# Attention blocks ahead of and beside a gated product: sums issued before maxima, four copies moved to ScalarE, the mask added on TensorE

## The chip, the core and the metric

The kernel runs on one core of one Trainium2 chip. The metric is the device time of one launch in microseconds. The engines are TensorE (matmuls, PE; its weight loads are PEld), VectorE (DVE), ScalarE (ACT), GpSimd (POOL) and the queue of SyncE (SP), from which most loads are issued. Each engine works through its own instructions in the order in which the kernel issues them.

## The reference

Three layers follow each other; all tensors are float32.

```
scores = q @ k^T / 8, only where 0 <= row - column < 64, else -1e9
attn   = exp(scores - max) / (sum(exp(scores - max)) + 1e-9);  x = attn @ v     # 4 x 8 heads, 576 rows, 64 wide
h = x @ w_in;  g = h * tanh(softplus(h));  y = g @ w_out                       # 2304 tokens, 512 -> 2048 -> 512
each token goes to its best of 8 experts: out = weight * relu(y @ w1[e]) @ w2[e]  # 512 -> 1024 -> 512
```

Since a row looks back over 64 columns at most, 64 rows need 128 columns of keys.

## The kernel before

The 2304 tokens make 36 attention blocks of 64 rows (`a`). A block holds all eight heads: four tiles (`KD`) of 128 x 128 scores, each with two heads on its 128 partitions. A block passes through stages that lie in different steps of the program (`na` counts the steps):

- `scores(a)`, step a: four float32 matmuls into one PSUM tile (L143). For a < 12 (`PRE`) a matmul of an identity with a bfloat16 mask is added ahead of them (L141), so the tile is already masked.
- `largest(a)`, step a+1: the row maxima. For a < 12 one DVE reduction over 128 x 512 in PSUM (L158) and a small POOL instruction that scales it (L159). From block 12 on, four DVE instructions of 128 x 128 each (L165), which add the mask, scale, write the result to SBUF and keep the minimum; they need no POOL instruction, and they free the PSUM tile.
- `exps(a)`, step a+1: four ACT exponentials, with the sums in `sm` (L183). For a < 12 they read PSUM, so the tile stays taken until they end.
- `scale(a)`, step a+2 (`LN`): a small POOL addition to the sums (L197), a DVE reciprocal (L198) and four POOL multiplications of 128 x 128 (L200).
- `flip(a)`, `flipped(a)`, `values(a)`, step a+3 (`LT`): four PE transposes (L210), a copy of their PSUM tile to SBUF (L215, by ACT for the steps in `PT_ACT`, else by DVE), eight pairs of products with v (L226).
- `done(a)`, step a+4: ACT copies the result out of PSUM (L238 or L244); for the first eight blocks `rest` takes a low part on DVE (L251).

Steps 0 to 11 are **attention alone** (`att_alone`). Its order is: loads, `done`, `largest(na-1)`, `scale(na-2)`, `flip(na-3)`, `scores(na)`, `flipped`, `rest`, `exps(na-1)`, conversions, `values(na-3)`. The conversions turn the 64-bit input weights of the gated layer into a high and a low 32-bit part: three DVE instructions (L299, L303, L307), an ACT cast (L325) and a DVE subtraction (L1003) for each of 32 pieces.

Then follow 28 **mixed** steps, one for each product step i of the gated layer: `hidden(i)` (24 matmuls into one of two PSUM tiles `h`; L337 to L341), `att_a`, the output product of step i-2 (12 matmuls; L376 to L378), `att_b`. The activation of h is spread over ACT and DVE: `mish_a` in `att_b` (L414 to L419), `mish_b` in the next `att_a` (`finish_mish`; L425 to L427), then the split of its result (L433, L434). L427 is the last reader of `h`; with two such tiles, `hidden(i)` waits for L427 of step i-2. In mixed steps `att_a` holds `largest(na-1)` and `scale(na-2)` ahead of `finish_mish`, and `scores(na)` is last in `att_b`. Conversions run until product step 13 (`CONV_END`).

Blocks with a < 12 alternate between two PSUM places for their scores; later blocks share one (`att_ps`, one buffer). The transposes of blocks from 9 on and all results `o` share another. The order is written out by hand (`manual_schedule`): no planner moves an instruction.

Of the kernel before, what the change touches and what calls it, by code (L numbers as in the profile page):

```python
# [11 lines left out]
F32 = mybir.dt.float32  # L12
# [12 lines left out]
P = 128  # L25
# [8 lines left out]
NB = NT // BLK  # L34
G = 256
NG = NT // G
KD = D // P
NEG = -8.0e9
LN, LT = 2, 3
PRE = 12  # L40
AHEAD = 1
PT_ACT = range(PRE, 27)
RAW_AT = -1, 1, 3
V_AT = 1
REST = range(NG)
# [24 lines left out]
class Attention:  # L70
# [59 lines left out]
    def scores(self, a):  # L130
        nc = self.nc
        g, j = divmod(a, 2)
        if a % 2 and a < PRE:
            s = self.spare.tile([P, KD, P], F32, name="s_acc", tag="acc1")
        else:
            s = self.ps.tile([P, KD, P], F32, name="s")
        masked = a < PRE
        if masked:
            mask = self.c["mask0_b"] if a % (S // BLK) == 0 else self.c["mask_b"]
            mask = mask.unsqueeze(1).broadcast_to([P, KD, P])  # L140
            nc.tensor.matmul(s, self.eye, mask, start=True, stop=False)  # L141
        for c in range(KD):
            nc.tensor.matmul(  # L143
                s[:, c, :],
                self.qd[g % 2][:, c].rearrange("p h (q j) -> p j (h q)", j=2)[:, j],
                self.kt[g][:, c, j * BLK : j * BLK + P],
                start=not masked,
                stop=not masked or c == KD - 1,
            )
        self.s[a] = s  # L150

    def largest(self, a):

        nc = self.nc
        s = self.s.pop(a)
        mx = self.pp.tile([P, KD], F32, name="mx")
        if a < PRE:
            nc.vector.tensor_reduce(out=mx, in_=s, op=ALU.max, axis=AX.X)  # L158
            nc.gpsimd.tensor_scalar(mx, mx, -1.0 / math.sqrt(HD), None, ALU.mult)  # L159
            self.p[a] = s, mx, 1.0 / math.sqrt(HD)  # L160
            return
        p = self.pp.tile([P, KD, P], F32, name="p")
        mask = self.c["mask0"] if a % (S // BLK) == 0 else self.c["mask"]
        for c in range(KD):
            nc.vector.tensor_tensor_reduce(  # L165
                out=p[:, c, :],
                in0=s[:, c, :],
                in1=mask,
                scale=-1.0 / math.sqrt(HD),
                scalar=3.0e38,  # L170
                op0=ALU.add,
                op1=ALU.min,
                accum_out=mx[:, c : c + 1],
            )
        self.p[a] = p, mx, -1.0

    def exps(self, a):
        nc = self.nc
        s, nm, scale = self.p[a]
        p = self.pp.tile([P, KD, P], F32, name="p") if a < PRE else s  # L180
        sm = self.pp.tile([P, KD], F32, name="sm")
        for c in range(KD):
            nc.scalar.activation(  # L183
                p[:, c, :],
                s[:, c, :],
                AF.Exp,
                scale=scale,
                bias=nm[:, c : c + 1],
                accum_out=sm[:, c : c + 1],
            )  # L190
        self.p[a] = p, sm
# [72 lines left out]
STEPS_ATT = NB + LT + 1  # L264
# [667 lines left out]
def tile_kernel(tc, a):  # L932
    nc = tc.nc
    with ExitStack() as ctx:
# [22 lines left out]
        with tc.manual_schedule():  # L957
# [4 lines left out]
            A = Attention(nc, att_ctx, tc, a["qT"], a["kT"], a["v"], a["x"], c, R.acc_ps, R.first_x)  # L962
# [21 lines left out]
            def convert_start(n):  # L984
                for _ in range(n):
                    if not under_way:
                        if not todo:
                            return
                        under_way.append((todo[0], R.convert_a(R.raws.pop(todo.pop(0)))))
                    key, parts = under_way[0]  # L990
                    f = next(parts)
                    if f is not None:
                        under_way.clear()
                        half_done.append((key, f))
                        fetch_next()
# [3 lines left out]
            def convert_end():  # L999
                def low():  # L1000
                    while low_parts:
                        key, args = low_parts.pop(0)
                        nc.vector.tensor_tensor(*args)  # L1003
                        ready.add(key)

                low()
                while half_done:
                    key, f = half_done.pop(0)
                    low_parts.append((key, R.convert_b(key, f)))
                if not todo and not under_way:  # L1010
                    low()

            na = 0

            def pt_copy():
                if na in PT_ACT:
                    return nc.scalar.copy
                return nc.vector.tensor_copy

            def att_a(convs, *between):  # L1020
                if A.on(na - LT - 1):
                    A.done(na - LT - 1)
                convert_end()
                convert_start(convs)
                if na < STEPS_ATT:
                    A.fetch(na)
                if A.on(na - 1):
                    A.largest(na - 1)
                if A.on(na - LN):
                    A.scale(na - LN)  # L1030
                A.rest()
                for f in between:
                    f()
                if A.on(na - LT):
                    A.flip(na - LT)

            def att_b(convs, *between):
                nonlocal na
                if A.on(na - LT):
                    A.flipped(na - LT, pt_copy())  # L1040
                convert_end()
                convert_start(convs)
                for f in between:
                    f()
                if A.on(na - 1):
                    A.exps(na - 1)
                if A.on(na - LT):
                    A.values(na - LT)
                if na < NB:
                    A.scores(na)  # L1050
                na += 1

            def att_alone(convs):
                nonlocal na
                A.fetch(na)
                if A.on(na - LT - 1):
                    A.done(na - LT - 1)
                if A.on(na - 1):
                    A.largest(na - 1)
                if A.on(na - LN):  # L1060
                    A.scale(na - LN)
                if A.on(na - LT):
                    A.flip(na - LT)
                A.scores(na)
                if A.on(na - LT):
                    A.flipped(na - LT, pt_copy())
                A.rest()
                if A.on(na - 1):
                    A.exps(na - 1)
                convert_end()  # L1070
                convert_start(convs)
                if A.on(na - LT):
                    A.values(na - LT)
                na += 1
# [14 lines left out]
            for i in range(PRE):  # L1089
                att_alone(PRE_CONV[i])  # L1090
                for _ in range(RAW_AT.count(i)):
                    fetch_next()
# [116 lines left out]
            for i in range(n + LAG):  # L1209
# [16 lines left out]
                if i < MIXED:  # L1226
                    att_a(CONV, finish_mish)
                else:
                    finish_mish()
# [34 lines left out]
                if i < MIXED:  # L1264
                    att_b(CONV, start_mish)
                else:
                    start_mish()
# [97 lines left out]
```

## Time and profile before

| | |
|---|---|
| median of 3 runs | 757.12 us (755.93 to 757.47) |
| profiled execution | 757.77 us, span 756.1 us |
| PE busy | 725.9 us, 96% |
| DVE busy | 557.0 us, 74% |
| ACT busy | 490.7 us, 65% |
| POOL busy | 244.2 us, 32% |
| mean granted TensorE clock | 0.995 |

Busy time is the time in which an engine runs instructions other than register, branch, semaphore and DMA-issuing ones. A share over the whole span says little here, since the stages have different limits. The first product step of the gated layer starts 45.10 us into the span; the mixed steps with conversions end near 157 us.

### The profile page before, as it was taken

The page shows a single profiled execution, that of the slowest core. Times are in us where ns is not written, and L with a number is a line of the kernel's source. Part 1 is how long each engine was busy: PE and PEld are TensorE (multiplying, and loading weights), DVE is VectorE, ACT ScalarE, POOL GpSimd, SP SyncE. Part 2 cuts the span into 40 slices and gives each one's busy share as a digit, 9 for nine tenths or more (in the row PEclk, how much of TensorE's full clock was granted, in tenths as well). Part 3 has the DMA queues.
Part 4 walks back from the last instruction along what each step waited for, and adds up shares of the span by engine and source line. Part 5 has one row for each costly group of instructions (what it writes and reads, how often), then busy time and mean ns, then how long its engine had stood idle before and what let it go on. Part 6 is the DMA issues. An engine that isn't in the chain of part 4 may idle for free. (4 is left out here: it accounts for less than half of the span.)

```text
span 756.1 us, 14103 instructions
## 1 busy us (share of the span) xinstructions
PE 725.9 (96%) x5109; PEld 647.6 (86%) x5109; DVE 557.0 (74%) x1389; ACT 490.7 (65%) x1018; POOL 244.2 (32%) x319
## 2 busy tenths in 40 slices
PE   6779999999999999999999999999989999999995
PEld 4568888888989899989988999988879998899994
DVE  4889999975655589889889898999895447643330
ACT  4568888898687677777777777776123546545461
POOL 5763333432323010110101101051424566565661
PEclk9999999999999999999999999999999999999998
DMA  8776666632322310100101001242011711111620
GB/s 267 246 227 232 208 209 220 221 119 78 109 87 72 126 31 1 56 17 15 57 1 57 15 15 64 78 148 75 29 57 56 264 43 44 42 56 43 206 74 32
DMA packets 42912, 75.51 MB, mean 100 GB/s; under 512 B 3857, under 2 KB 20241, under 8 KB 42706
## 3 DMA queue, kind: packets, MB, share of 16 engines
q1 hardware_dynamic: 30818, 56.01, 23.2%
q0 software_dynamic: 4480, 14.46, 5.7%
q10 hardware_dynamic: 7536, 4.06, 1.9%
q8 instruction: 42, 0.69, 0.4%
q14 instruction: 36, 0.29, 0.1%
HBM read 82.36 MB, written 13.39 MB: 127 GB/s over the span
## 5 line engine op out<-in xcount | busy, mean ns | idle before, releaser
L337 PE MATMUL h<-xh,w 128*128 128x256 f32 x576 | 165.9, 288 | 0.8 <-DVE y L427 0.5
L341 PE MATMUL h<-xh,w 128*128 128x256 f32 x576 | 162.8, 283 | 0.0
L340 PE MATMUL h<-xl,w 128*128 128x256 f32 x576 | 162.8, 283 | 0.0
L376 PE MATMUL acc<-w,g 128*128 128x512 f32 x288 | 115.5, 401 | 0.0
L337 PEld LDWEIGHTS h<-xh,w 128*128 128x128 f32 x576 | 110.0, 191 | 6.0 <-DVE y L427 3.3
L377 PE MATMUL acc<-w,g 128*128 128x512 f32 x288 | 112.7, 391 | 0.0
L378 PE MATMUL acc<-w,g 128*128 128x512 f32 x288 | 112.6, 391 | 0.0
L340 PEld LDWEIGHTS h<-xl,w 128*128 128x128 f32 x576 | 110.2, 191 | 1.4
L200 POOL TENSOR_SCALAR p<-p,r 128x128 f32<-128x128 f32 x144 | 84.2, 601 | 80.9 <-DVE r L198 80.9
L341 PEld LDWEIGHTS h<-xh,w 128*128 128x128 f32 x576 | 110.1, 191 | 0.0
L549 DVE CUSTOM_DVE_ANT_0 junk<-row,wg 128x512 bf16<-128x512 f32 x144 | 105.7, 734 | 2.7
L628 POOL DMA_INDIRECT xs_dram<-row,posi x18 | 20.3, 1127 | 215.2 <-DVE row L619 97.2
L873 POOL TENSOR_TENSOR ew<-s,ew 128x1024 fp32r<-128x1024 f32 x32 | 80.0, 2514 | 27.7 <-ACT ew L872 27.5
L441 ACT ACTIVATE g<-h 128x512 fp32r<-128x512 f32 x36 | 21.5, 598 | 100.9 <-PE h L341 100.9
L340 PE MATMUL h<-xl,ew 128*128 128x256 f32 x288 | 82.5, 286 | 1.5 <-DVE xl L907 1.5
L337 PE MATMUL h<-xh,ew 128*128 128x256 f32 x288 | 82.3, 286 | 0.5 <-DVE g L442 0.5
L341 PE MATMUL h<-xh,ew 128*128 128x256 f32 x288 | 82.2, 285 | 0.0
L414 ACT ACTIVATE y<-h 128x512 f32<-128x512 f32 x72 | 43.0, 597 | 56.9 <-PE h L341 53.7
L419 DVE SCALAR_TENSOR_TENSOR pq<-y,r 128x512 f32<-128x512 f32 x72 | 49.9, 693 | 36.7 <-ACT r L417 36.7
L865 DVE TENSOR_TENSOR ew<-s,ew 128x1024 fp32r<-128x1024 f32 x32 | 55.1, 1721 | 25.3 <-ACT ew L864 25.1
L442 DVE SCALAR_TENSOR_TENSOR g<-h,g 128x512 fp32r<-128x512 f32 x36 | 24.8, 689 | 62.4 <-ACT g L441 62.3
L425 ACT ACTIVATE pq<-pq,mid 128x512 f32<-128x512 f32 x72 | 52.1, 723 | 27.5 <-DVE pq L419 23.3
(216 smaller groups left out, 1704.3 us busy)
## 6 DMA issues: line engine op xcount, KB each, us to landing
s<-e_w SPq DMA_DIRECT2D x32, 1024.0 KB
v<-v SPq DMA_DIRECT2D x36, 256.0 KB
raw<-w_in SPq DMA_DIRECT2D x16, 512.0 KB
raw<-w_out SPq DMA_DIRECT2D x16, 512.0 KB
kt<-kT SPq DMA_DIRECT2D x17, 384.0 KB
qd<-qT SPq DMA_DIRECT2D x36, 128.0 KB
x_dram<-xs ACTq DMA_DIRECT2D x14, 256.0 KB
xraw<-x_dram SPq DMA_DIRECT2D x14, 256.0 KB
```

The lines of the kernel that those rows point to most:

```text
L200: nc.gpsimd.tensor_scalar(p[:, c, :], p[:, c, :], r[:, c : c + 1], 0.0, ALU.mult, ALU.add)
L337: nc.tensor.matmul(h[:, f], w[:, 0, k, fs], xh[:, k], start=(k == 0), stop=False)
L340: nc.tensor.matmul(h[:, f], w[:, 0, k, fs], xl[:, k], start=False, stop=False)
L341: nc.tensor.matmul(h[:, f], w[:, 1, k, fs], xh[:, k], start=False, stop=(k == KD - 1))
L376: nc.tensor.matmul(acc[c], gh[:, 0, f, cs], w[:, 0, f], start=st, stop=False)
L377: nc.tensor.matmul(acc[c], gh[:, 0, f, cs], w[:, 1, f], start=False, stop=False)
L378: nc.tensor.matmul(acc[c], gh[:, 1, f, cs], w[:, 0, f], start=False, stop=en)
L419: nc.vector.scalar_tensor_tensor(p, y, 1.0, r, ALU.add, ALU.mult)
L425: nc.scalar.activation(p, p, AF.Square, bias=self.c["mid"][:, 0:1])
L549: nc.vector.tensor_tensor_reduce(out=junk, in0=rows[c][:, 0:D], in1=self.wg[:, e], scale=1.0, scalar=0.0, op0=ALU.mult, op1=ALU.add, accum ...
L865: nc.vector.tensor_tensor(t[:, 1], src, t[:, 0].bitcast(F32), ALU.subtract)
L873: nc.gpsimd.tensor_tensor(t[:, 1], src, t[:, 0].bitcast(F32), ALU.subtract)
```

## The change

For blocks 12 to 25 too, the mask is added by a matmul with the identity; their maxima become one DVE reduction and one POOL instruction, and their exponentials read PSUM (`MASK_PE`). In `att_alone`, `scale(na-2)` is issued ahead of `largest(na-1)`. In the steps 4, 6, 8 and 10 the copy of the transposes is done by ACT instead of DVE. In mixed steps `scores(na-1)` is issued in the next step's `att_a`, behind its `hidden`, where `scores(na)` was last in `att_b`; the loads (`fetch`) are issued behind it; and `largest` moves from the head of `att_a` into `att_b`, behind `flipped`, so that it now follows `finish_mish`.

```diff
+MASK_PE = 26
-PT_ACT = range(PRE, 27)
+PT_ACT = 4, 6, 8, 10, *range(PRE, 27)
 # scores, largest, exps:
-        masked = a < PRE
+        masked = a < MASK_PE
-        if a < PRE:
+        if a < MASK_PE:
-        p = self.pp.tile([P, KD, P], F32, name="p") if a < PRE else s
+        p = self.pp.tile([P, KD, P], F32, name="p") if a < MASK_PE else s
 # att_a:
                 convert_start(convs)
-                if na < STEPS_ATT:
-                    A.fetch(na)
-                if A.on(na - 1):
-                    A.largest(na - 1)
                 if A.on(na - LN):
                     A.scale(na - LN)
                 A.rest()
+                if A.on(na - 1) and na > PRE:
+                    A.scores(na - 1)
+                if na < STEPS_ATT:
+                    A.fetch(na)
                 for f in between:
                     f()
 # att_b:
                     A.flipped(na - LT, pt_copy())
+                if A.on(na - 1):
+                    A.largest(na - 1)
                 convert_end()
...
                     A.values(na - LT)
-                if na < NB:
-                    A.scores(na)
                 na += 1
 # att_alone:
+                if A.on(na - LN):
+                    A.scale(na - LN)
                 if A.on(na - 1):
                     A.largest(na - 1)
-                if A.on(na - LN):
-                    A.scale(na - LN)
```

## Rows read from the trace of the kernel before

**Rows 1.** Busy time by stage: length, each engine's busy us, clock, DMA share, GB/s.

```profile
5.20:45.10 39.90, 30.89 (x288) 24.42 (x288) 26.82 (x57) 21.60 (x100) 26.07 (x60) 1.00 0.86 268
45.10:66.89 21.79, 18.50 (x172) 16.68 (x169) 20.12 (x50) 17.43 (x43) 10.30 (x17) 1.00 0.71 221
66.89:157.09 90.20, 89.98 (x708) 77.61 (x706) 89.10 (x231) 77.68 (x199) 32.48 (x57) 1.00 0.65 206
157.09:164.90 7.81, 7.81 (x67) 6.97 (x66) 4.79 (x15) 7.46 (x23) 2.61 (x6) 1.00 0.56 187
```

**Rows 2.** Timeline of POOL in the steps alone: start, us, instruction, idle before.

```profile
12.55 1.43 POOL L200 TENSOR_SCALAR p<-p,r 128x128 f32<-128x128 f32 x4 [0.31 <-DVE r L198]
...
17.33 1.93 POOL L200 TENSOR_SCALAR p<-p,r 128x128 f32<-128x128 f32 x4 [0.31 <-DVE r L198]
...
23.80 2.37 POOL L200 TENSOR_SCALAR p<-p,r 128x128 f32<-128x128 f32 x4 [0.38 <-DVE r L198]
26.70 0.23 POOL L159 TENSOR_SCALAR mx<-mx 128x4 f32<-128x4 f32 x1 [0.52 <-DVE mx L158]
27.01 0.23 POOL L197 TENSOR_SCALAR r<-sm 128x4 f32<-128x4 f32 x1
27.62 2.64 POOL L200 TENSOR_SCALAR p<-p,r 128x128 f32<-128x128 f32 x4 [0.38 <-DVE r L198]
...
31.70 2.61 POOL L200 TENSOR_SCALAR p<-p,r 128x128 f32<-128x128 f32 x4 [0.38 <-DVE r L198]
...
39.57 2.64 POOL L200 TENSOR_SCALAR p<-p,r 128x128 f32<-128x128 f32 x4 [0.38 <-DVE r L198]
```

**Rows 3.** Timeline of DVE in the steps alone and the first mixed step.

```profile
27.27 0.18 DVE L198 RECIPROCAL r<-r 128x4 f32<-128x4 f32 x1 [0.73 <-POOL r L197]
27.36 0.66 DVE L215 COPY pt<-t_acc 128x512 f32<-128x512 f32 x1
27.94 0.41 DVE L251 TENSOR_TENSOR xl<-o,xh 128x256 fp32r<-128x256 f32 x1
28.27 0.68 DVE L1003 TENSOR_TENSOR w<-cv,w 128x512 fp32r<-128x512 f32 x1
...
29.94 0.68 DVE L158 TENSOR_REDUCE mx<-s_acc 128x4 f32<-128x512 f32 x1
...
43.40 0.66 DVE L215 COPY pt<-t_acc 128x512 f32<-128x512 f32 x1
...
49.92 0.18 DVE L198 RECIPROCAL r<-r 128x4 f32<-128x4 f32 x1 [0.73 <-POOL r L197]
```

**Rows 4.** Timeline of ACT in the steps alone: ends of exponentials, and their start.

```profile
11.16 0.21 ACT L183 ACTIVATION_READ_ACCUMULATOR p<-s,mx 128x1 f32 x1
...
26.96 0.37 ACT L183 ACTIVATE p<-s,mx 128x128 f32<-128x128 f32 x1 [1.20 <-POOL mx L159]
...
28.25 0.21 ACT L183 ACTIVATION_READ_ACCUMULATOR p<-s,mx 128x1 f32 x1
```

**Rows 5.** Timeline of a mixed step: last sum on ACT, then POOL.

```profile
93.51 0.19 ACT L183 ACTIVATION_READ_ACCUMULATOR p<-p,mx 128x1 f32 x1
...
93.85 0.23 POOL L197 TENSOR_SCALAR r<-sm 128x4 f32<-128x4 f32 x1 [0.85 <-ACT p L183]
```

**Rows 6.** Timeline of DVE in a mixed step: first masked maximum and what follows.

```profile
89.17 0.28 DVE L165 CUSTOM_DVE_ANT_0 p<-s,mask 128x128 f32<-128x128 f32 x1
...
90.01 0.17 DVE L198 RECIPROCAL r<-r 128x4 f32<-128x4 f32 x1
```

**Rows 7.** Who waited for whom, 45 to 160 us: us in total, times, longest.

```profile
PEld h L337 <- DVE y L427: 2.1, 10, 0.2
```

**Rows 8.** Timeline of PE: mask, scores; transposes behind the first product step.

```profile
42.43 0.38 PE L141 MATMUL s_acc<-mask_b,eye 128*128 128x512 bf16 x1
42.65 1.10 PE L143 MATMUL s_acc<-kt,qd 128*128 128x128 f32 x8
...
48.08 0.60 PE L210 MATMUL t<-ident,p 128*128 128x128 f32 x4
```

## The prediction

> **What bounds the kernel now.** I read the busy time by stage first, then the timelines of the single engines inside a stage. The stages have three limits. In the steps alone no engine is full: of 39.90 us PE is busy 30.89, DVE 26.82, POOL 26.07 [rows 1]; a step is limited by a round trip, seen below. In the mixed steps with conversions DVE is full: 89.10 of 90.20 us in eleven steps, 8.20 us each [rows 1], and the list of waits has ten of these products wait for the last DVE reader of `h` [rows 7]. From 157 us on the mixed steps are PE's: 7.81 busy of 7.81 us [rows 1]. Since PE is never idle from there, a shift of the first product step (45.10 us) is carried to the end unless the mixed steps with conversions give it back. So the sum is made of three terms.
>
> **Term A, the steps alone: the order of sums and maxima.** Before, POOL runs the small maximum instruction of block na-1 (L159, 26.70 us), then the sum instruction of block na-2 (L197, 27.01), then the four scalings (L200, 27.62 to 30.26) [rows 2]. The exponentials of block na-1 start at 26.96 us, beside the scalings of the block before [rows 2, 4]: exponentials and scalings overlap, and DVE pays only 0.73 us of waiting for the sum in each step [rows 3]. POOL keeps the program's order. In the new order it runs sum, four scalings, and only then the maximum instruction of the next block, for which the next exponentials wait, whose sums the next scalings need. That closes a ring in which nothing of two blocks overlaps:
>
> - L159 to the first exponential: 26.70 to 26.96, 0.26 us [rows 2, 4];
> - exponentials to the end of the last sum: 26.96 to 28.46, 1.50 us [rows 4];
> - from there to L197: 93.70 to 93.85, 0.15 us [rows 5];
> - L197 to the first scaling, with the reciprocal between: 27.01 to 27.62, 0.61 us [rows 2];
> - the scalings: 1.43 us at best, up to 2.64 us [rows 2];
> - L159 right behind the last of them: taken at nothing.
>
> One pass is 2.52 us plus the scalings, so 3.95 us at least. How long the scalings take is set by what DVE runs beside them. With DVE in a PSUM copy and a PSUM subtraction (27.36 to 28.35) and then in instructions on two SBUF tiles (from 28.27), they take 2.64 us, while the first four of all, with almost nothing of that kind beside them, take 1.43 [rows 2, 3]. In the new order DVE runs reciprocal, maximum (0.68, the next one can start 0.08 sooner, so 0.60), copy (0.58 likewise), subtraction (0.33), then the SBUF work [rows 3]: 1.51 us of PSUM work covers scalings of 1.43. In the steps 4, 6, 8 and 10 the copy is gone to ACT and the cover is 0.93 us, as before the change (0.91); for these I take the measured 1.93, 2.37, 2.61 and 2.64 us of the same steps [rows 2], for the other five 1.43. The copies on ACT cost nothing themselves, since ACT idles before the exponentials (1.20 us at 26.96 [rows 4]).
>
> The first sum can start 0.15 us after the last sum of block 0 (11.16 + 0.21), at 11.52 us [rows 4]. Nine passes lead to the sum of block 9: 9 x 2.52 + 5 x 1.43 + 9.55 = 39.4, so 50.9 us. Then come the reciprocal (0.26 later, 27.01 to 27.27 [rows 2, 3]), 0.09 for it, the maximum (0.60) and the copy of block 8, at 51.85 us. Before it stands at 43.40 [rows 3], and the last products with v and the first product step follow it in both. **A = +8.45 us**. Bounds: +4.6 with 1.43 in all passes (9.55 - 4 x 1.43 = 3.83 less); +12.1 with 2.64 also in the three passes of steps 5, 7 and 9 (3 x 1.21).
>
> What this hinges on at its upper end is whether a maximum beside scalings leaves them alone. The Trainium skill (SBUF, "Who interferes with whom") says that on trn2 a `tensor_reduce` never contends with GpSimd, while an instruction with two SBUF inputs does. By that rule the sum stays at +8.45; if the maximum blocked scalings as the SBUF instructions of these rows do, it would be +12.1.
>
> **Term B, the first three mixed steps** (45.10 to 66.89, 21.79 us with DVE busy 20.12 [rows 1]). DVE works through a queue; product step 3 starts when L427 of step 1 ends. Ahead of that L427 the change takes away: the four masked maxima of block 13, which now stand behind it (89.17 to 90.01, 0.84 us [rows 6]); 0.24 us of block 12's (0.84 becomes one reduction of 0.60); and the wait of 0.73 us for the sum behind the maximum instruction, which the first mixed step still had [rows 3]. **B = -1.8 us**. Bounds: nothing, if something else holds L427, and -3.3, the distance to the 18.50 us that PE is busy there [rows 1].
>
> **Term C, the eleven steps to 157.09.** DVE saves 0.24 us in each, 8.20 to 7.96. PE gains a mask matmul: the scores behind it start 42.65 - 42.43 = 0.22 us later [rows 8], so its floor rises from 7.81 to 8.03 us. PE is late next: 11 x (8.03 - 8.20) = **-1.9 us**, and one mask falls into the first PE-bound step behind them, **+0.2**. Bounds: no better than -1.9, since 8.03 is PE's work; no gain at all is +0.2, and PE stalls could add to that (second rival).
>
> The rest costs nothing, by cover. The loads, now behind the scores on SP with the second half's weight loads behind them, come some 4 us later (2.98 for `hidden`, 1.0 for the scores [rows 8]) for data used two steps, 16 us, on. Unmasked maxima behind L427 (blocks 26 on) meet a DVE busy 4.79 of 7.81 us [rows 1].
>
> Sum: 8.45 - 1.8 - 1.9 + 0.2 = +4.95 us on the profiled 757.77, 762.7; that execution lies 0.65 above the median of the runs, so **762.1 us**.
>
> **Rivals.** *The cheap ring.* All scalings at 1.43: A = +4.6, sum +1.1, 758.2 us on the median. For it: the maximum and the subtraction read PSUM. Against it: the four steps with the copy on ACT give the cover away that 2.64 us was measured with.
>
> *Stalled scores.* From block 12 on one PSUM tile serves all scores, and with masks on TensorE it is free only when the exponentials end, not when the maximum does. In DVE's pace the maximum follows L427 at once: 0.68 [rows 3], an estimated 0.4 to the exponentials (0.26 from L159 on and a signal to it like the 0.15 above), 1.50 for them [rows 4]: 2.6 us after L427, while the scores come some 3.0 us after it, behind `hidden` (45.10 to 48.08 [rows 8]). The margin is 0.4 us. If queues on POOL and ACT eat it and a quarter of a microsecond more in each of twelve steps, B and C are lost and 3 us are added: 757.1 + 8.45 + 3 = 768.5 us.
>
> *DVE relieved.* The ring doesn't decide; the steps alone stay at DVE's pace, which loses 0.73 us of waiting in nine steps and 0.58 in four, 8.9 us, of which POOL's own work (3.5 of a step of some 4.05: 2.64 + 0.61 + 0.23) lets 0.5 through in the six long steps: -3. With B and C 757.1 - 3 - 3.5 = 750.6 us. It decides if the maximum instruction reaches ACT before the scalings. Against it stands the order on POOL in every step of [rows 2]. The Trainium skill (Perfetto Trace Analysis, "Optimizing Scalar/DVE Operations") says that with DVE saturated it may make sense to offload some work to Scalar; the four copies would then be 2.3 us of this gain. Here DVE is busy 26.82 of 39.90 us in that stage [rows 1], so I give this little.
>
> **How the numbers follow.** Forecast (759.5 to 766) 0.62; cheap ring 0.16; stalled scores 0.13; DVE relieved 0.09. Within 0.2%, 1.5 us, a measurement can't tell a change. The cheap ring lies on the edge: of its 0.16 I give 0.12 to the same. The range, 757.3 to 767.0 us, takes in the ring's lower bound and most of its upper one; left out are the relieved DVE and most of the stalled scores. Faster 0.09, same 0.12, slower 0.79.
>
> **What would show it.** After the change POOL's L159 must follow the fourth scaling without a gap in the steps alone, the exponentials must lie between the last L159 and the next L197, and the scalings must be longer in steps 4, 6, 8 and 10 than in their neighbours. The first product step must start near 53.5 us, the product steps from the fourth on must be 8.03 to 8.1 us apart, and the wait of `hidden` for L427 be gone. A first product step before 46 us would make the forecast wrong, a step of 8.2 us or more would make term C wrong.

## The result, and the profile after

The changed kernel takes 767.74 us (765.52 to 768.85) against 757.23 (755.93 to 757.47): a ratio of 1.0139, interval 1.0111 to 1.0167. Slower was forecast, at 762.1; the time lies 0.7 us above the range, and the loss is twice the one forecast. The lines of the new kernel are one higher than those of the old.

The profiled executions are 757.77 and 768.85 us, the second 1.1 us above its kernel's median; their spans differ by 11.0 us. Four stretches carry it: the start of the first product step moves from 45.10 to 54.22 us (+9.1), the first three product steps grow from 21.78 to 24.06 (+2.3), the next eleven shrink from 90.20 to 88.29 (-1.9), and what follows grows from 598.97 to 600.46 (+1.5). Busy time by stage of the kernel after answers to [rows 1] (columns as there):

```profile
5.20:54.22 49.02, 34.95 (x288) 29.10 (x288) 24.52 (x54) 21.56 (x99) 24.96 (x61) 0.87 0.73 217
54.22:78.28 24.06, 21.27 (x164) 19.54 (x162) 19.28 (x37) 18.29 (x50) 9.87 (x18) 0.83 0.65 206
78.28:166.57 88.29, 88.29 (x719) 78.48 (x715) 84.46 (x153) 76.66 (x199) 27.46 (x67) 1.00 0.66 209
174.60:182.39 7.79, 7.79 (x68) 6.97 (x64) 5.73 (x17) 7.10 (x22) 2.14 (x5) 1.00 0.56 172
```

The eleven steps are PE's now, 88.29 of 88.29 us. New is the clock column: 0.87 and 0.83 in the first two stages, 1.00 before.

**The ring.** POOL's timeline of the kernel after, steps 5 to 7 and the end of the ring, answers to [rows 2]:

```profile
22.42 0.23 POOL L198 TENSOR_SCALAR r<-sm 128x4 f32<-128x4 f32 x1 [1.70 <-ACT p L184]
23.03 1.42 POOL L201 TENSOR_SCALAR p<-p,r 128x128 f32<-128x128 f32 x4 [0.39 <-DVE r L199]
24.42 0.94 POOL L160 TENSOR_SCALAR mx<-mx 128x4 f32<-128x4 f32 x1
27.06 0.23 POOL L198 TENSOR_SCALAR r<-sm 128x4 f32<-128x4 f32 x1 [1.70 <-ACT p L184]
27.66 2.35 POOL L201 TENSOR_SCALAR p<-p,r 128x128 f32<-128x128 f32 x4 [0.38 <-DVE r L199]
29.99 0.22 POOL L160 TENSOR_SCALAR mx<-mx 128x4 f32<-128x4 f32 x1
...
51.12 0.23 POOL L198 TENSOR_SCALAR r<-sm 128x4 f32<-128x4 f32 x1 [1.70 <-ACT p L184]
```

The maximum instruction follows the fourth scaling without a gap, and then POOL idles 1.62 to 1.70 us for the exponentials in every pass. In a step with the copy on DVE the scalings take 1.42 us (1.65 in one), in one with the copy on ACT 2.35, as taken. Not taken: in this DVE-copy step the small instruction, 0.22 us alone, takes 0.94, beside DVE's SBUF work (0.94, 0.94 and 0.65 in three of nine passes).

**The clock.** Stretches of the kernel after, columns as in the stages, then the first three product steps one by one, and a wait of PE:

```profile
20.00:24.00 4.00, 2.06 (x21) 1.64 (x16) 1.35 (x5) 1.77 (x9) 1.92 (x7) 1.00 0.56 142
24.00:27.00 3.00, 2.05 (x21) 1.65 (x21) 1.32 (x4) 1.60 (x9) 1.36 (x3) 0.62 0.23 71
36.00:40.00 4.00, 3.57 (x27) 3.13 (x27) 2.73 (x6) 1.67 (x7) 3.02 (x6) 0.50 0.15 26
54.20:59.40 5.20, 5.20 (x28) 5.18 (x27) 5.10 (x11) 1.89 (x9) 2.98 (x4) 0.55 0.67 205
59.40:68.70 9.30, 6.58 (x73) 5.74 (x71) 5.21 (x11) 7.99 (x21) 3.86 (x8) 1.00 0.66 191
...
54.22:61.17 6.95, 6.22 (x47) 5.92 (x45) 5.87 (x12) 3.13 (x12) 4.24 (x6) 0.67 0.74 231
61.17:68.77 7.60, 5.54 (x58) 5.01 (x54) 4.49 (x9) 6.80 (x19) 2.67 (x5) 1.00 0.61 166
68.77:78.28 9.51, 9.51 (x65) 8.62 (x65) 8.93 (x17) 8.36 (x21) 2.95 (x8) 0.82 0.62 219
...
24.47 0.95 PE L227 MATMUL o<-pt,v 128*64 128x64 f32 x16 [2.40 <-issue]
```

From 20 to 24 us PE is busy 2.06 of 4.00 us at full clock, and it waits 2.40 us ahead of the products at 24.47; behind that the clock is 0.62, and later 0.50, which is 1.2 GHz for the whole stretch. The first product step falls into such a stretch: its 24 matmuls take 5.16 us instead of 3.14. Behind them stand the transposes, behind those the copy in ACT's queue, behind that the activation of `h`, and DVE waits for its end (timelines of ACT and DVE after):

```profile
59.91 0.58 ACT L216 COPY pt<-t 128x512 f32<-128x512 f32 x1 [3.82 <-PE t L211]
63.63 0.69 DVE L420 SCALAR_TENSOR_TENSOR pq<-y,r 128x512 f32<-128x512 f32 x1 [3.41 <-ACT r L418]
```

### The profile page after: what moved, and what is told of

The parts are those of the page before. It is cut to its first block, busy times and chain, and to the rows that moved or that the text cites. A ratio compares the mean times of both kernels' runs of the same rounds, so it can differ in the third digit from the quotient of the medians.

```text
span 767.0 us, 14072 instructions
## 1 busy us (share of the span) xinstructions
PE 732.1 (95%) x5123; PEld 657.1 (86%) x5123; DVE 555.5 (72%) x1287; ACT 491.0 (64%) x1022; POOL 235.6 (31%) x333
## 5 line engine op out<-in xcount | busy, mean ns | idle before, releaser
L338 PE MATMUL h<-xh,w 128*128 128x256 f32 x576 | 167.9, 291 | 1.0 <-DVE y L428 0.9
L342 PE MATMUL h<-xh,w 128*128 128x256 f32 x576 | 164.5, 286 | 0.0
L341 PE MATMUL h<-xl,w 128*128 128x256 f32 x576 | 164.5, 286 | 0.0
L338 PEld LDWEIGHTS h<-xh,w 128*128 128x128 f32 x576 | 112.0, 194 | 6.1 <-DVE y L428 1.7
L341 PEld LDWEIGHTS h<-xl,w 128*128 128x128 f32 x576 | 112.0, 194 | 1.4
L342 PEld LDWEIGHTS h<-xh,w 128*128 128x128 f32 x576 | 112.0, 194 | 0.0
L874 POOL TENSOR_TENSOR ew<-s,ew 128x1024 fp32r<-128x1024 f32 x32 | 79.5, 2498 | 29.2 <-ACT ew L873 29.0
L442 ACT ACTIVATE g<-h 128x512 fp32r<-128x512 f32 x36 | 21.5, 598 | 101.0 <-PE h L342 101.0
L201 POOL TENSOR_SCALAR p<-p,r 128x128 f32<-128x128 f32 x144 | 66.3, 476 | 57.6 <-DVE r L199 55.3
L866 DVE TENSOR_TENSOR ew<-s,ew 128x1024 fp32r<-128x1024 f32 x32 | 61.9, 1934 | 22.7 <-ACT ew L865 22.6
```

The lines of the kernel that those rows point to most:

```text
L201: nc.gpsimd.tensor_scalar(p[:, c, :], p[:, c, :], r[:, c : c + 1], 0.0, ALU.mult, ALU.add)
L338: nc.tensor.matmul(h[:, f], w[:, 0, k, fs], xh[:, k], start=(k == 0), stop=False)
L341: nc.tensor.matmul(h[:, f], w[:, 0, k, fs], xl[:, k], start=False, stop=False)
L342: nc.tensor.matmul(h[:, f], w[:, 1, k, fs], xh[:, k], start=False, stop=(k == KD - 1))
L866: nc.vector.tensor_tensor(t[:, 1], src, t[:, 0].bitcast(F32), ALU.subtract)
L874: nc.gpsimd.tensor_tensor(t[:, 1], src, t[:, 0].bitcast(F32), ALU.subtract)
```

## The experiments

The theory is that the new order alone closes the ring (A), that PE idling in it loses the clock and with it the gain of the first product steps, and that the mixed part of the change is worth some 3 us. The first rival is that the mixed part costs; the second that the clock is a sign and no cost. Ratios are to the kernel before in runs on the same chip.

### e1: the old order in the steps alone

```diff
 # the changed kernel, att_alone:
+                if A.on(na - 1):
+                    A.largest(na - 1)
                 if A.on(na - LN):
                     A.scale(na - LN)
-                if A.on(na - 1):
-                    A.largest(na - 1)
```

> The changed kernel with the steps alone in the old order again (maxima ahead of sums); the four copies on ACT and the whole change to the mixed steps stay. Theory (the new order closes a ring on POOL, ACT and DVE, and the idle TensorE then loses its clock): first product step at 42 to 44 us, clock 1.00 throughout, product steps from the fourth on 8.03 us, first three product steps 20 to 21 us; 751 to 753 us. Rival (the mixed part of the change, the late scores and their one PSUM tile, is what costs): 760 us or more, with the first product step near 45 us and slow steps behind it.

Measured: 754.43 us (751.95 to 756.83), ratio 0.996 (0.9943 to 0.9977). The median is 1.4 us above the expected time. By stage:

```profile
5.20:42.67 37.47, 31.68 (x288) 24.44 (x289) 24.69 (x53) 23.18 (x104) 26.12 (x62) 1.00 0.93 278
42.67:63.66 20.99, 17.91 (x165) 16.09 (x163) 18.81 (x36) 17.33 (x43) 8.23 (x17) 1.00 0.74 228
63.66:151.95 88.29, 88.29 (x719) 78.48 (x715) 85.25 (x155) 76.98 (x199) 29.51 (x68) 1.00 0.66 213
```

The first product step starts at 42.67, the clock is 1.00 in all three stages, and the eleven steps take the same 88.29 us: the loss lies in this one swap. The mixed part gains: 20.99 and 88.29 us in these two stages against 21.78 and 90.20 before, 2.7 us, of which 1.0 is given back in the eleven steps behind them (85.96 against 84.98 us). With the ring gone, exponentials and scalings overlap again (timelines of ACT and POOL):

```profile
25.09 0.37 ACT L184 ACTIVATE p<-s,mx 128x128 f32<-128x128 f32 x1 [0.61 <-POOL mx L160]
25.14 0.23 POOL L198 TENSOR_SCALAR r<-sm 128x4 f32<-128x4 f32 x1
25.75 2.65 POOL L201 TENSOR_SCALAR p<-p,r 128x128 f32<-128x128 f32 x4 [0.38 <-DVE r L199]
```

Counted from the first L159 or L160, the steps alone take 33.7 us here (8.94 to 42.67), 35.5 before (9.59 to 45.10) and 45.8 after (8.42 to 54.22). So in the old order the four copies on ACT are worth 1.8 us, and the new order costs 12.1 in these steps against e1.

### e2: the new order alone, in the kernel before

```diff
 # the kernel before, att_alone:
-                if A.on(na - 1):
-                    A.largest(na - 1)
                 if A.on(na - LN):
                     A.scale(na - LN)
+                if A.on(na - 1):
+                    A.largest(na - 1)
```

> The kernel before with one edit: in the steps alone the sums are issued ahead of the maxima. Copies stay on DVE, mixed steps as before. Theory: the ring is there, with scalings of 1.43 us in all passes but POOL's small maximum instruction sometimes held up by DVE; first product step at 49 to 53 us, granted clock below 1 somewhere between 20 and 70 us; 763 to 768 us. Rival (the mixed part costs): 756 to 759 us.

Measured: 765.04 us (764.4 to 765.55), ratio 1.0102 (1.0085 to 1.0119); first product step at 53.03 us, mean clock 0.987. POOL's timeline:

```profile
33.02 1.42 POOL L200 TENSOR_SCALAR p<-p,r 128x128 f32<-128x128 f32 x4 [0.38 <-DVE r L198]
34.41 0.94 POOL L159 TENSOR_SCALAR mx<-mx 128x4 f32<-128x4 f32 x1
37.05 0.23 POOL L197 TENSOR_SCALAR r<-sm 128x4 f32<-128x4 f32 x1 [1.70 <-ACT p L183]
```

Seven of nine passes have L159 at 0.65 to 0.94 us, and eight of them scalings of 1.42 to 1.47. From the first sum to that of block 9 the ring takes 39.1 us (11.27 to 50.38), against 40.8 with four copies on ACT (10.29 to 51.12). The copies cost the ring 1.7 us, not the 3.8 that their longer scalings suggest: what DVE does not take from the scalings it takes from the small instruction. The mixed steps of this kernel are those of the kernel before, and yet its first three product steps are 2.0 us longer, at a clock of 0.86:

```profile
53.03:76.82 23.79, 21.30 (x172) 19.66 (x169) 20.31 (x50) 19.22 (x52) 8.58 (x16) 0.86 0.64 209
```

### e3: the new order, with the small instruction on DVE

```diff
 # the changed kernel, largest:
-            nc.gpsimd.tensor_scalar(mx, mx, -1.0 / math.sqrt(HD), None, ALU.mult)
+            eng = nc.vector if a < PRE else nc.gpsimd
+            eng.tensor_scalar(mx, mx, -1.0 / math.sqrt(HD), None, ALU.mult)
```

> The changed kernel, but for blocks 0 to 11 the small instruction that scales the maxima runs on DVE right behind the reduction instead of on POOL. The new order stays. Theory (what closes the ring is that this instruction stands behind the scalings in POOL's queue): the exponentials no longer wait for scalings, first product step at 42 to 45 us, clock 1.00; 750 to 754 us. Rival (issuing the sums first costs by itself, since DVE's reciprocal then waits for the exponentials ahead of the maximum): the ring stays nearly as long, 762 us or more.

Measured: 753.56 us (753.12 to 754.63), ratio 0.9951 (0.9934 to 0.9967); first product step at 43.22, first three product steps 21.01 us. The order of sums and maxima is the changed one; only the place in POOL's queue is gone, and with it the ring. Issuing sums first is not free even so: in e8, below, which differs in the order of these two calls alone, the first product step starts 2.3 us earlier, at 40.96. In total the two can't be told apart (0.9951 and 0.9949).

### e4, e6, e9: the changed kernel with TensorE kept busier

```diff
 # the changed kernel, att_alone, from step 2 on:
                 A.scores(na)
+                spin(5)          # e9: 3
...
                     A.values(na - LT)
+                spin(3)          # e9: 2
+ # spin(n): n matmuls of the identity with the mask, 512 columns, into a tile of h_ps
```

> The changed kernel with eight matmuls of the identity with the mask (bfloat16, 512 columns) added to each of the steps 2 to 11, into a PSUM tile nobody reads, so that TensorE idles less there. Theory (ring plus clock): the ring stays, first product step at 52 to 55 us, but the clock stays at 1.00 and the first three product steps take 20 to 22 us instead of 24; 762 to 765 us. Rival (the clock is only a sign and costs nothing): 767 to 770 us.

> The changed kernel with eight idle matmuls in each of the steps 2 to 11, again. In the first profile of it the clock stayed up and the first three product steps took 21.6 instead of 24.1 us, but its time was not shorter: 2 us went into waits of the expert stage, which the change does not touch. Theory (those waits come and go by themselves): now 1.5 to 3 us below the changed kernel beside it. Rival (matmuls kept busy early cost as much later, by whatever way): within 1 us of it or above.

> The changed kernel with five idle matmuls in each of the steps 2 to 11 instead of eight. With eight, the first three product steps were 2.0 to 2.5 us shorter, but in both profiles one DVE subtraction of the expert stage then stood 6.1 us behind POOL instead of 2.7, which gave the time back. Theory (that hold-up hangs on the moment at which DVE and POOL meet there, not on the clock): clock 0.99 or more, first three product steps 21 to 22 us; where the hold-up does not come, 764.5 to 766.5 us. Rival (a busier start always costs that much later): 768 to 770 us.

Beside them ran e5, the changed kernel again.

> The changed kernel once more, on one chip with the kernels beside it, so that the clock's share is read from one set of runs. All theories: 765.5 to 769 us, first three product steps near 24 us, granted clock 0.98.

Measured: e4 768.76 us (767.59 to 772.55), ratio 1.0164 (1.0131 to 1.0197); e6 769.76 (768.31 to 771.53), 1.0181 (1.0162 to 1.02); e5, on the chip of e6, 768.07 (767.07 to 768.55), 1.0154 (1.0137 to 1.017); e9 766.64 (764.72 to 767.49), 1.0119 (1.0101 to 1.0137). e4 and e6 missed the theory's times, and in total the second rival's came: 767 to 770 for e4, and for e6 no less than the changed kernel beside it. The stages are the theory's. In e4, e6 and e9 the first product step starts at 54.79, 55.05 and 55.17 us, behind 0.25 to 0.47 us of idle matmuls, and in e5 at 54.79, so the ring does not depend on the clock; the first three product steps take 21.10, 21.07 and 21.95 us against 23.54 in e5. A stretch of e6 in the steps alone, then these three steps:

```profile
30.00:40.00 10.00, 8.81 (x89) 6.10 (x90) 6.31 (x14) 5.05 (x21) 5.84 (x13) 1.00 0.59 187
...
55.05:60.06 5.01, 4.28 (x47) 3.95 (x45) 4.91 (x11) 3.10 (x12) 2.85 (x4) 1.00 0.70 182
60.06:67.67 7.61, 5.55 (x58) 5.00 (x54) 5.42 (x11) 6.81 (x19) 4.08 (x8) 1.00 0.97 242
67.67:76.12 8.45, 8.18 (x65) 7.20 (x65) 7.87 (x15) 8.24 (x21) 2.09 (x7) 1.00 0.64 213
```

Against the changed kernel (6.95, 7.60 and 9.51 us at 0.67, 1.00 and 0.82) the two steps with a reduced clock are shorter, 1.9 and 1.1 us, and the one at full clock is not. So the clock costs 3.0 us there in the first profile and 2.5 in e5; 2.5 and 2.0 if the idle matmuls ahead of the first step are counted in.

What e6 lost again lies 540 us later, in the expert stage that the change does not touch: 2.2 us at one DVE subtraction, and 0.6 where the same line is held up once more, at 663 us (6.26 us for 1.23). DVE's timeline at the first of them, e5, then e6:

```profile
594.55 2.68 DVE L866 TENSOR_TENSOR ew<-s,ew 128x1024 fp32r<-128x1024 f32 x1 [0.68 <-ACT ew L865]
```

```profile
592.16 6.08 DVE L866 TENSOR_TENSOR ew<-s,ew 128x1024 fp32r<-128x1024 f32 x1 [0.67 <-ACT ew L865]
```

This subtraction of two SBUF tiles takes 1.22 us undisturbed. In e5 it takes 2.68, and the two POOL products beside it (L874) 5.85 together; in e6, and likewise in e4 (6.07), the two POOL products run back to back in 4.78 us right behind DVE's start, DVE gets through only after both, and `hidden` then waits 2.1 to 2.5 us. In e9 it takes 2.68 at this place. The kernel before has such hold-ups at other places (up to 6.29 us for the same line), so the change does not create them; that they hang on the moment of meeting fits the profiles, and what sets that moment, and so whether a kept clock brings them on, was not tried. e9's time, 766.64 us, is just above the 764.5 to 766.5 expected: the third of its first product steps still takes 9.34 us for 8.45, partly at the reduced clock. So the clock's cost is shown for these steps; for the whole kernel e9 alone points to it, and its interval touches that of e5.

### e7: masks of the later blocks back on DVE

```diff
 # e1, and:
-MASK_PE = 26
+MASK_PE = PRE
```

> The changed kernel with the steps alone in the old order and without masks on TensorE from block 12 on (four masked maxima on DVE, as before the change); the late scores, the late maxima and the four copies on ACT stay. Theory (term C is VectorE's saving, bought with a 0.22 us matmul): product steps from the fourth on 8.15 to 8.25 us instead of 8.03, eleven of them 90 us, 754 to 756 us, 1.5 to 2 us above the kernel with old order and masks on TensorE (751 to 755 us). Rival (the place of scores and maxima alone gives the gain): steps of 8.0 us or less, 750 to 753 us.

Measured: 752.39 us (752.03 to 753.97), ratio 0.9952 (0.9936 to 0.9967): not slower than e1 (0.9943 to 0.9977), and the rival's step of 8.0 us came. First three and next eleven product steps:

```profile
43.83:65.21 21.38, 18.80 (x164) 17.09 (x161) 19.31 (x47) 17.58 (x43) 7.89 (x16) 0.92 0.70 217
65.21:152.32 87.11, 86.25 (x708) 76.65 (x705) 86.01 (x234) 78.74 (x198) 26.37 (x56) 1.00 0.68 215
```

The eleven steps are 1.18 us shorter than with masks on TensorE, with all four masked maxima on DVE. Why DVE has room shows in the same DVE groups of the kernel before (its steps 66.89 to 157.09) and of e7 (mean ns behind the comma):

```profile
L1003 DVE TENSOR_TENSOR w<-cv,w 128x512 fp32r<-128x512 f32 x24 | 18.2, 760 | 0.0
...
L299 DVE TENSOR_SCALAR cv<-raw 128x512 int32<-128x512 int32 x21 | 9.9, 471 | 0.0
```

```profile
L1004 DVE TENSOR_TENSOR w<-cv,w 128x512 fp32r<-128x512 f32 x23 | 15.7, 685 | 0.0
...
L300 DVE TENSOR_SCALAR cv<-raw 128x512 int32<-128x512 int32 x21 | 8.8, 420 | 0.0
```

In the eleven steps 24 x 0.075 + 21 x 0.051 = 2.9 us, 0.26 in a step, are the whole way from 8.23 to 7.97. The scalings moved: before, they ran into the conversions; with the maxima behind L427 they fall beside instructions that read PSUM. POOL in a step of the kernel before, then of e7:

```profile
90.35 2.65 POOL L200 TENSOR_SCALAR p<-p,r 128x128 f32<-128x128 f32 x4 [4.49 <-DVE r L198]
```

```profile
103.47 1.70 POOL L201 TENSOR_SCALAR p<-p,r 128x128 f32<-128x128 f32 x4 [3.65 <-DVE r L199]
```

### e8, e10: what paid, together

```diff
 # e8: e1 with the edit of e3
 # e10: e8, and:
-MASK_PE = 26
+MASK_PE = PRE
```

> The changed kernel with the steps alone in the old order, and the small factor on the maxima of blocks 0 to 11 on DVE. It takes away both that the maxima wait for POOL and DVE's wait of 0.73 us for the sum. Theory (in the old order the steps alone are paced by DVE's work and that wait): first product step at 39 to 41 us, 748 to 752 us. Rival (in the old order POOL's scalings pace the steps, and they grow as DVE gets denser): first product step at 42 to 43 us, no faster than with either edit alone, 752 to 755 us.

> What paid, together: steps alone in the old order, factor on the maxima on DVE for blocks 0 to 11, four copies on ACT, masks of later blocks on DVE, scores and maxima late in the mixed steps. Theory (the terms add): first product step at 40.5 to 42 us, first three product steps 21.0 to 21.5, the next eleven 87.1 us; 749 to 752 us. Rival (a gain early is lost later): 752 to 755 us.

Measured: e8 752.06 us (750.38 to 755.5), ratio 0.9949 (0.9931 to 0.9968), first product step at 40.96 as the theory says, though the time is just inside the rival's and in total e8 cannot be told from e1, e3 or e7. e10 takes 751.5 us (750.09 to 751.79), ratio 0.9917 (0.9903 to 0.9931): faster than both kernels, by 0.8% and, ratio to ratio, 2.2%. Its stages:

```profile
5.20:41.09 35.89, 31.37 (x288) 25.12 (x288) 26.78 (x64) 24.36 (x105) 23.29 (x49) 0.95 0.99 291
41.09:62.55 21.46, 18.75 (x163) 17.04 (x161) 19.56 (x47) 17.60 (x43) 8.79 (x17) 0.92 0.71 230
62.55:149.63 87.08, 86.21 (x709) 76.59 (x705) 85.98 (x234) 78.70 (x198) 26.32 (x56) 1.00 0.68 215
```

The clock is below 1.00 in two stages here too, and in the second of them in e7 and e11, without the ring; what that costs was not tried.

### e11: late maxima, scores left at the end of the step

```diff
 # e7, and:
-                if A.on(na - 1) and na > PRE:
-                    A.scores(na - 1)
 # att_b, behind values, as before the change (fetch back too):
+                if na < NB:
+                    A.scores(na)
```

> Old order in the steps alone, four copies on ACT, masks on DVE, and of the mixed steps only the maxima moved behind the last reader of h: the scores stay at the end of the step, the loads where they were. Theory (the gain of the mixed steps comes from where the maxima stand: POOL's scalings then fall beside DVE instructions that read PSUM): product steps 7.95 to 8.05 us as with late scores, 751 to 754 us. Rival (the late maxima need the late scores, since the scores of the next block wait in TensorE's queue for the one PSUM tile that the maxima free): product steps of 8.3 us or more, 755 us or more.

Measured: 756.96 us (756.01 to 758.36), ratio 0.9998 (0.9989 to 1.0007), no gain on the kernel before. The rival's time came, and the theory's steps (88.04 us for eleven, 8.04 in the even run of them). The loss lies in the first three product steps: 24.37 us, 3.0 more than in e7. The first is 0.97 longer, since one block's scores lie in it again, as before the change. The second takes 9.21 us for 7.61; the scores wait 0.90 there for the maxima, and the clock is 0.81. The third takes 9.28 for 8.85, with PE busy throughout, at 0.82. In the even steps the wait that the rival named is there, but small (60 to 160 us):

```profile
PEld s L144 <- DVE mx L166: 2.7, 9, 0.3
PE s L144 <- DVE mx L166: 1.1, 7, 0.2
```

So the late maxima paid only with the late scores. How much of the 3.0 us is this wait and how much clock (0.86 in that stage, 0.92 in e7) was not tried.

## Why the prediction was wrong

- **Term A held as a mechanism and was 0.7 us too small**: +9.1 for +8.45. The first maximum came 1.2 us earlier than before, which e5 (9.43) shows to differ between executions; so the 0.7 is partly luck, and counted from the first maximum the stage grew by 10.3. From the first sum to that of block 9 the ring took 40.83 us for 39.4: L160 behind DVE's SBUF work adds 1.87 in three passes, where the working had "taken at nothing" for the place behind the scalings and 0.26 for the instruction itself; other pieces came out 0.4 shorter. From the copy of block 8 (52.05) to the first product step it took 2.17 for 1.70 us, the products with v at half clock. The scalings beside the maximum took 1.42 us: there the trace agrees with the Trainium skill (SBUF, "Who interferes with whom"), by which a reduction leaves GpSimd alone.
- **Term B is the step that failed**: "-1.8 us", with bounds of nothing and -3.3, and +2.3 came. Its working counted DVE's queue alone and took PE's own work at the durations of the kernel before. No sentence, bound or rival had PE's clock in it, though by term A PE had the same work in 8.45 us more. With the clock kept up the stage takes 21.1 us (21.5 with the idle matmuls ahead of it), with the old order 21.0: so 2.5 to 3.1 us of the miss of 4.1 are clock. The rest, 1.0 to 1.6, is gain that did not come even at full clock. In e1 DVE, with less in its queue, waits for ACT ahead of the last reader of `h` in the first product step, where the working had it busy without a break:

```profile
50.05 0.69 DVE L420 SCALAR_TENSOR_TENSOR pq<-y,r 128x512 f32<-128x512 f32 x1 [0.80 <-ACT r L418]
...
53.62 0.72 DVE L427 SCALAR_TENSOR_TENSOR pq<-pq,r 128x512 f32<-128x512 f32 x1 [0.52 <-ACT pq L426]
```

- **Term C came out to the size, for part of the reason.** The steps are 8.03 us and PE's, 88.29 us in all; PE sets that size, whatever more DVE saves. But the working gave DVE's saving to the single reduction. DVE is busy 89.10 us in the eleven steps before, 84.46 after, and 86.01 in e7, which keeps the four masked maxima: two thirds of the saving come without the reduction, and DVE comes down to 7.97 a step. That the place beside the scalings does it is read from the groups above, and e11, with the maxima alone moved, has steps of 8.04. In these steps the mask on TensorE buys nothing: it puts PE's floor at 8.03 us, above the 7.97 that DVE reaches without it.
- **The last +0.2 was +1.5.** The masked step gave 0.2. The scores, moved behind `hidden`, stand one step later, so one block's scores leave the first three product steps, where DVE sets the pace, and come into the 25th, where PE does (7.79 us for 6.85): the working had no term for it. With the 0.02 us that each step between is shorter, the two make 1.0 by the end of that step. The remaining 0.5 lies in the expert stage, in hold-ups like that of e6, and is -0.2 in e5. There PE is not "never idle from there": in the kernel before it is busy throughout from 157 to 242 us, but idles 11.9 of the last 244.1 us.
- **The rivals.** Stalled scores fell: eleven even steps of 8.03 us. The cheap ring fell on the long scalings. DVE relieved fell in the changed kernel, but its condition, that the maxima reach ACT ahead of the scalings, is what e3 makes true, and there 753.6 us came.

## What to carry to other kernels

A small instruction that another engine waits for must not stand behind long ones in an in-order queue: before swapping two calls, write down for each engine what ends up behind what, and look for a ring through several of them; here moving one 128x4 instruction to another engine undid the loss. Where a change makes TensorE idle longer ahead of dense work, look at the granted clock of that stretch and price the work behind it at half speed as a rival of its own. And an operation can be worth moving for what runs beside it: two thirds of what looked like saved VectorE work came with the new place beside GpSimd's.

## What the runs showed of the hardware

- GpSimd's smallest instructions suffer too, not only its long ones: 128x4 took 0.22 us alone and 0.65 to 0.94 beside DVE's SBUF work.
- It goes both ways: a DVE subtraction of two SBUF tiles (128x1024) takes 1.22 us undisturbed; in e6 it started 0.2 us ahead of two POOL products in a row, and took 6.08.
- The granted clock fell to 1.2 GHz in stretches of the steps alone of the changed kernel, behind waits of PE of 2.40 us; in the kernel before, whose longest wait after 12 us of these steps is 0.76 us, it stayed at 2.4 GHz.
- The last wait alone does not tell: behind one of 1.66 us in the second product step the clock fell to 1.2 GHz in e7 and stayed at 2.4 GHz in e1. What makes the difference was not tried.
